# v of chunks 0 to 3 of batch 0 loaded through ScalarE's DMA queue instead of SyncE's

## The chip, the cores and the metric

The kernel runs on one NeuronCore of a Trainium2 chip. The core has TensorE (matrix products and transposes into PSUM), VectorE, ScalarE and GpSimd (elementwise work), and SyncE, which here only issues transfers. In the profile they are PE (PEld for its weight loads), DVE, ACT, POOL and SP. The metric is the device time of one execution in microseconds (us); lower is better.

## The reference

Four batches, eight heads, 768 tokens, head dimension 64; the heads side by side make rows of 512.

```python
gamma = 1.0 - 2.0 ** (-5.0 - np.arange(H))          # one decay per head
for t in range(S):
    state = gamma * state + einsum('bhd,bhe->bhde', k[:, :, t], v[:, :, t])
    y[:, :, t] = scale * einsum('bhd,bhde->bhe', q[:, :, t], state)
x = y.transpose(0, 2, 1, 3).reshape(B, S, H * D)
h = x.transpose(0, 2, 1) @ U @ V                    # rank 32, over tokens
u = x + h.transpose(0, 2, 1)
out = u + np.maximum(u @ w_ch1, 0.0) @ w_ch2        # 512 -> 2048 -> 512
```

A recurrent attention is followed by a low-rank mixing of tokens and a two-layer network on each token.

## The kernel before

The recurrence is computed in six chunks of 128 tokens (`NCK`). Within a chunk, q and k are scaled by powers of the decay (`ret_q0`, `ret_k`, giving `qd` and `kd` in bf16), transposed on TensorE (`ret_Tq0`, `ret_Tk0`), and multiplied to scores (`ret_S`), which VectorE masks (`ret_mask`). v is cast to bf16 by ScalarE (`ret_v`). `ret_sum` adds the chunk's k times v to the state in PSUM, `ret_state` takes a masked copy of it, and `ret_O` forms the chunk's output x from the masked scores with v and from the state with q. Then `mix_x`, `mix_P` and `mix_h` form u transposed, and `mlp1` and `mlp2` are the two layers.

For batches 1 to 3 the recurrence is woven into the two layers of the batch before. Batch 0 has nothing to be woven into: its recurrence stands in the open, in an order written out by hand in lines 574 to 649, with matmuls on zeros (`run_idle`) in places where TensorE would wait. `manual_schedule` keeps each engine's instructions in the order of the source. Each engine takes its own in order.

What the change and the prediction touch:

- Lines 178 to 188: SyncE issues batch 0's loads in the order k0, q0, k1, q1, k2, V, k3, v0, q2, k4, v1, k5, v2, v3, v4, v5, U. `k`c and `v`c are chunk c (256 KB each); `q`i is a pair of chunks (512 KB), so q0, q1, q2 of this list are chunks 0 and 1, 2 and 3, 4 and 5. V is moe_V and U moe_U, 96 KB each.
- `load_one` (line 136) makes the tile and issues the load. The pool `rin` has six buffers for each of k, q and v, so that batch 0's loads wait for no buffer.
- `ret_Tk0` (line 334) transposes the scaled k of a chunk; ScalarE copies the result out of PSUM as `kT` for chunks 0 to 3 and VectorE for 4 and 5. `ret_Tq0` (line 316) does so for a pair of q; of the first pair VectorE copies one half and ScalarE the other, of the later pairs ScalarE copies both in one instruction. Both copies by ScalarE have line 312.
- `ret_v` (line 274) casts v of a chunk on ScalarE; it waits for that v.
- Line 613: a small copy on GpSimd from v of chunk 4 stands ahead of the weight loads in GpSimd's own queue, so that these start when v4 has landed.

Of the kernel before, what the change touches and what calls it, by code (L numbers as in the profile page):

```python
# [47 lines left out]
def kernel(  # L48
# [11 lines left out]
    nc = tc.nc  # L60
    P = 128
# [28 lines left out]
    def bank(i, dtype=fp32, free=DM):  # L90
        n_bank[0] += 1
        return psum.tile([P, free], dtype, tag=f"bk{i}", name=f"bk{i}_{n_bank[0]}")
# [21 lines left out]
    def matmul(o, l, r, cols, **kw):  # L114
        nc.tensor.matmul(o, l, r, **kw)  # L115
        bal.mm(cols)
# [15 lines left out]
    staged = {}  # L132

    gate = (1, 0)

    def load_one(t, b, c, src, nm):
        n = rin.tile([P, H, D], fp32, tag=nm, name=f"{nm}_{b}_{c}")
        if (b, c) == gate:
            nc.scalar.activation(n[:, 0, :1], lsc, AF.Copy)
        nc.sync.dma_start(out=n, in_=src[b, :, ts(c, P), :].rearrange("h p d -> p h d"))  # L140
        t[nm, c] = n

    def load_chunk(b, c):
        t = {}
        for src, nm in ((k, "k_n"), (q, "q_n"), (v, "v_n")):
            load_one(t, b, c, src, nm)
        staged[b, c] = (t["q_n", c], t["k_n", c], t["v_n", c])
# [23 lines left out]
    t0 = {}  # L171

    def load_q0(i):
        t0["q", i] = q0f[:, i]
        nc.sync.dma_start(out=q0f[:, i].rearrange("p h e d -> p h (e d)"),
                          in_=q[0, :, ds(2 * P * i, 2 * P)].rearrange("h (p e) d -> p h (e d)", e=2))

    for what in ("k0", "q0", "k1", "q1", "k2", "V", "k3", "v0", "q2", "k4", "v1", "k5", "v2", "v3",
                 "v4", "v5"):
        if what == "V":  # L180
            nc.sync.dma_start(out=Vf, in_=moe_V)
        elif what[0] == "q":
            load_q0(int(what[1]))
        else:
            load_one(t0, 0, int(what[1]), k if what[0] == "k" else v, what[0] + "_n")
    for c in range(NCK):
        staged[0, c] = (None, t0["k_n", c], t0["v_n", c])
    nc.sync.dma_start(out=Uf, in_=moe_U.rearrange("(j p) r -> p j r", p=P))


# [3 lines left out]
    def run_idle(n):  # L194
        w = bank(0)
        for _ in range(n):
            matmul(w, idle[:, :P], idle, DM, start=True, stop=True)
# [50 lines left out]
    def cast_v():  # L248
        nc.vector.tensor_copy(out=Vs, in_=Vf)
# [8 lines left out]

    xs, rc = {}, {}
    st_p = {}  # L260

    def ret_k(b, c, eng):
        q_n, k_n, v_n = staged.pop((b, c))
        kd = rmid.tile([P, H, D], bf16, tag="kd", name=f"kd_{b}_{c}", bufs=6)
        eng.tensor_tensor(kd, k_n, Gk[:, c].unsqueeze(2).to_broadcast([P, H, D]), op=ALU.mult)  # L265
        rc[b, c] = dict(kd=kd, q_n=q_n, v_n=v_n)
# [22 lines left out]
    def by_dma(b):  # L289
        return b >= 2  # L290
# [11 lines left out]
    def ret_q0(i, eng):  # L302
        t0["qd", i] = []
        for e in (0, 1):
            d = rmid.tile([P, H, D], bf16, tag="qd", name=f"qd0_{i}_{e}", bufs=4)
            eng[e].tensor_tensor(d, t0["q", i][:, :, e],  # L306
                                 Gq0[:, 2 * i + e].unsqueeze(2).to_broadcast([P, H, D]), op=ALU.mult)
            t0["qd", i].append(d)

    def copy_by(eng, o, i):  # L310
        if eng == "A":
            nc.scalar.activation(o, i, AF.Copy)  # L312
        else:
            nc.vector.tensor_copy(out=o, in_=i)

    def ret_Tq0(i, bks, between=0):

        tp = [bank(bk, bf16, 2 * DM) for bk in bks]
        o = q0T[:, :, ds(2 * P * i, 2 * P)].rearrange("p n (t e) -> p e n t", e=2)
        for e, d in enumerate(t0["qd", i]):  # L320
            t = tp[e % len(tp)]
            if e and between:
                run_idle(between)
            for n in range(NP):
                nc.tensor.transpose(t[:, ds((e if len(tp) == 1 else 0) * DM + n * P, P)],
                                    d[:, ds(2 * n, 2)], ident)
                bal.mm(P)
        if len(tp) == 2:
            for e, eng in ((0, "V"), (1, "A")):
                copy_by(eng, o[:, e], tp[e][:, :DM].rearrange("p (n t) -> p n t", n=NP))  # L330
        else:
            copy_by("A", o, tp[0].rearrange("p (e n t) -> p e n t", e=2, n=NP))

    def ret_Tk0(c, eng="A"):
        r = rc[0, c]
        o = rmid.tile([P, NP, P], bf16, tag="qkT", name=f"kT_0_{c}", bufs=6)
        tp = bank((2, TP)[c % 2], bf16, 2 * DM)[:, :DM]
        for p in range(NP):
            nc.tensor.transpose(tp[:, ts(p, P)], r["kd"][:, ds(2 * p, 2)], ident)
            bal.mm(P)  # L340
        r["kT"], r["qT"] = o, q0T[:, :, ts(c, P)]
        copy_by(eng, o.rearrange("p n t -> p (n t)"), tp)
# [14 lines left out]
    def ret_S(b, cs, masks=True, bks=(SA, SB)):  # L357

        for c, bks in zip(cs, (bks, (OB, TP if by_dma(b) else 2))):
            r = rc[b, c]  # L360
            r["s"] = [bank(i) for i in bks]
            for p in range(NP):
                for e in (0, 1):
                    matmul(r["s"][e][:, ts(p, P)], r["kT"][ds(D * e, D), p],
                           r["qT"][ds(D * e, D), p], 80, start=True, stop=True)
        for c in cs:
            rc[b, c]["a"] = rmid.tile([P, 2, NP, P], bf16, tag="a", name=f"a_{b}_{c}", bufs=5)
            for e in (0, 1) if masks else ():
                ret_mask(b, c, e)

    def ret_mask(b, c, e):
        r = rc[b, c]
        nc.vector.tensor_tensor(r["a"][:, e], r["s"][e].rearrange("p (n t) -> p n t", n=NP), mask4,  # L373
                                op=ALU.mult)
        bal.book("V", 0.69)
# [196 lines left out]
    G, V = nc.gpsimd, nc.vector  # L572

    ret_k(0, 0, G)
    ret_Tk0(0)
    run_idle(6)
    ret_q0(0, (V, G))
    ret_Tq0(0, (1, OB), 3)
    run_idle(3)
    ret_k(0, 1, G)  # L580
    ret_q0(1, (G, V))
    ret_Tk0(1)
    ret_S(0, [0])
    run_idle(4)
    ret_Tq0(1, (1,))
    ret_k(0, 2, G)
    ret_Tk0(2)
    ret_S(0, [1], bks=(OB, ST))
    cast_v()
    run_idle(4)  # L590
# [128 lines left out]
```

## Time and profile before

| what | us |
|---|---|
| median of 3 runs | 229.44 |
| lowest, highest run | 229.36, 230.59 |
| span of the profiled execution | 227.7 |
| TensorE busy in the span | 220.0 |
| ScalarE busy | 114.0 |
| VectorE busy | 82.3 |
| GpSimd busy | 55.4 |

The span runs from the first to the last instruction in the trace; the profiled execution has no other time of its own, and the median of the runs lies 1.74 us above its span. SPq is SyncE's sequencer, which issues the loads: the length of an SPq row is the time that the issue held it, not the transfer. The time from the issue's start to the landing of the data stands in the view of transfers. A row of a timeline has start, length, engine, line, operation, output and inputs, count, and in brackets the idle time of the engine before it with what ended that.

### The profile page before, as it was taken

Reading aid. Unit: us, or ns where it says so; the run is one execution under the profiler, and the core shown is the slowest. Engines: PE = TensorE matmul, PEld = TensorE weight load, DVE = VectorE, ACT = ScalarE, POOL = GpSimd, SP = SyncE. Lnnn points to the kernel's source line nnn. Section 1 sums busy time; section 2 is a strip of 40 time slices with the busy share of each in tenths; the row PEclk is TensorE's granted clock in tenths of the full one; section 3 lists DMA queues with packets and bytes.
Section 4 is the critical chain, followed back from the end, with each engine's and each line's share of the span. In section 5 each row is a group of like instructions: output and inputs, shape, how many; then the busy total and the mean of one; then the engine's idle time right before and its main releaser. Section 6 shows DMA issues by size and latency. Waiting matters only on the chain.

```text
span 227.7 us, 4234 instructions
## 1 busy us (share of the span) xinstructions
PE 220.0 (97%) x1713; PEld 123.9 (54%) x1713; DVE 82.3 (36%) x155; ACT 114.0 (50%) x219; POOL 55.4 (24%) x63
## 2 busy tenths in 40 slices
PE   7898899999999999999999999999999999999995
PEld 2455666655566456656554445655554456654454
DVE  5587620003776440015673710035674510001221
ACT  4366777761336377767232627767134457770000
POOL 3852910026655330522035501050000000000000
DMA  7999899999999997987599959859311550001122
GB/s 177 241 242 202 112 193 206 201 208 228 219 210 270 211 243 188 196 168 100 105 236 236 250 132 217 202 101 94 94 49 46 135 146 0 0 0 49 61 79 92
DMA packets 102324, 34.95 MB, mean 154 GB/s; under 512 B 91264, under 2 KB 99328, under 8 KB 102304
## 3 DMA queue, kind: packets, MB, share of 16 engines
q1 hardware_dynamic: 97552, 30.49, 63.9%
q0 software_dynamic: 4752, 4.19, 11.7%
q8 instruction: 13, 0.21, 0.4%
q14 instruction: 7, 0.06, 0.1%
HBM read 27.46 MB, written 6.29 MB: 148 GB/s over the span
## 4 chain that ended last, share of the span: by engine, by line
PE 77%; SPq 7%; DMA 7%; DVE 3%; ACT 1%; issue 1%; POOL 1%; POOLq 0%
PE bk L115 75%; SPq L140 3%; DMA q0f<-in_q_dram 3%; SPq L296 2%; DMA qkT<-kd 2%; DVE a L373 1%; PE bk L351 1%; DMA qkT<-qd 1%; DMA uT<-x 1%; SPq L520 1%; DVE res L517 1%; DVE state L417 1%; POOL qd L306 1%; ACT q0T L312 1%; POOL kd L265 1%
## 5 line engine op out<-in xcount | busy, mean ns | idle before, releaser
L115 PE MATMUL bk<-w2b,gT 128*128 128x512 bf16 (+2 forms) x416 | 92.0, 363 | 0.0
L115 PE MATMUL bk<-uT,w1b 128*128 128x384 bf16 x512 | 84.5, 326 | 0.5 <-DMA uT<-x 0.5
L120 ACT ACTIVATE gT<-bk 128x384 bf16<-128x384 f32 x126 | 61.7, 490 | 31.8 <-PE bk L115 31.7
L115 PEld LDWEIGHTS <-w1b 128*128 128x128 bf16 x512 | 49.8, 98 | 34.3 <-issue 1.5
L115 PEld LDWEIGHTS <-gT 128*128 128x128 bf16 x416 | 37.9, 98 | 37.8 <-issue 0.8
L373 DVE TENSOR_TENSOR a<-bk,mask 128x512 bf16<-128x512 f32 x48 | 30.1, 683 | 40.4 <-PE bk L115 40.2
L265 POOL TENSOR_TENSOR kd<-k_n,Gk 128x512 bf16<-128x512 f32 x24 | 25.0, 1042 | 79.9 <-PE bk L115 47.2
L517 DVE TENSOR_TENSOR res<-bk,res 128x512 f32<-128x512 f32 (+2 forms) x17 | 10.7, 626 | 44.9 <-PE bk L115 44.9
L395 ACT ACTIVATE x<-bk 128x512 bf16<-128x512 f32 x23 | 13.7, 595 | 25.2 <-PE bk L115 25.2
L270 POOL TENSOR_TENSOR qd<-q_n,Gq 128x512 bf16<-128x512 f32 x18 | 18.7, 1042 | 10.5 <-DMA qkT<-qd 9.3
L417 DVE TENSOR_TENSOR state<-bk,bmask 128x512 bf16<-128x512 f32 x20 | 13.8, 691 | 12.5 <-PE bk L115 12.4
L276 ACT ACTIVATE vb<-v_n 128x512 bf16<-128x512 f32 x24 | 14.6, 623 | 2.2 <-DMA v_n<-in_v_dram 2.2
L115 PE MATMUL bk<-idle 128*128 128x512 bf16 x41 | 12.4, 430 | 1.2 <-DVE idle L192 1.2
L484 DVE TENSOR_TENSOR res<-bk,x 128x512 f32<-128x512 f32 x15 | 9.7, 686 | 8.0 <-PE bk L115 8.0
L486 ACT ACTIVATE x<-res 128x512 bf16<-128x512 f32 x15 | 9.3, 630 | 6.8 <-DVE res L484 6.5
L115 PEld LDWEIGHTS <-qkT 64*128 64x128 bf16 (+1 forms) x204 | 8.4, 95 | 7.4 <-issue 3.2
L124 DVE COPY qkT<-bk 128x1024 bf16<-128x1024 bf16 x3 | 2.1, 692 | 26.4 <-PE bk L351 26.4
L115 PE MATMUL bk<-vb,a 128*128 128x64 bf16 x192 | 9.5, 193 | 0.0
L115 PE MATMUL bk<-P_sb,Vb 128*128 128x512 bf16 x24 | 9.1, 380 | 0.0
L115 PE MATMUL bk<-vb,kd 128*128 128x128 bf16 x80 | 7.8, 219 | 1.2 <-DVE state L417 0.9
L120 ACT ACTIVATE qkT<-bk 128x1024 bf16<-128x1024 bf16 x3 | 3.1, 1023 | 11.3 <-PE bk L351 11.3
L115 PEld LDWEIGHTS <-a 128*128 128x128 bf16 x192 | 8.0, 98 | 0.6
(72 smaller groups left out, 104.9 us busy)
## 6 DMA issues: line engine op xcount, KB each, us to landing
k_n<-in_k_dram SPq DMA_DIRECT2D x24, 256.0 KB, 4.9
v_n<-in_v_dram SPq DMA_DIRECT2D x24, 256.0 KB, 5.1
out_dram<-res SPq DMA_DIRECT2D x23, 256.0 KB, 2.5
q_n<-in_q_dram SPq DMA_DIRECT2D x18, 256.0 KB, 5.0
w2b<-in_moe_w_ch_dram POOLq DMA_DIRECT2D x4, 512.0 KB, 17.3
q0f<-in_q_dram SPq DMA_DIRECT2D x3, 512.0 KB, 6.1
w1b<-in_moe_w_ch_dram POOLq DMA_DIRECT2D x3, 512.0 KB, 9.6
w1b<-in_moe_w_ch_dram POOLq DMA_DIRECT2D x2, 256.0 KB, 5.0
```

The source lines that it names most:

```text
L115: nc.tensor.matmul(o, l, r, **kw)
L120: nc.scalar.activation(o, i, AF.Relu if relu else AF.Copy)
L140: nc.sync.dma_start(out=n, in_=src[b, :, ts(c, P), :].rearrange("h p d -> p h d"))
L265: eng.tensor_tensor(kd, k_n, Gk[:, c].unsqueeze(2).to_broadcast([P, H, D]), op=ALU.mult)
L270: eng.tensor_tensor(qd, rc[b, c]["q_n"], Gq[:, c].unsqueeze(2).to_broadcast([P, H, D]), op=ALU.mult)
L276: nc.scalar.activation(vb, rc[b, c]["v_n"], AF.Copy)
L373: nc.vector.tensor_tensor(r["a"][:, e], r["s"][e].rearrange("p (n t) -> p n t", n=NP), mask4, op=ALU.mult)
L395: nc.scalar.activation(xs[b][:, c], o[0], AF.Copy)
L417: nc.vector.tensor_tensor(sb, ps.rearrange("p (n t) -> p n t", n=NP), bmask4, op=ALU.mult)
L484: nc.vector.tensor_tensor(u, h, xs[b][:, j], op=ALU.add)
L486: nc.scalar.activation(xs[b][:, j], u, AF.Copy)
L517: nc.vector.tensor_tensor(o, chp.pop((b, j)), o if by_token(b, j) else xs[b][:, j, ds(lo, w)], op=ALU.add)
```

## The change

`load_one` gets an argument for the engine that issues, SyncE if none is given. SyncE's list loses v0 to v3. A new function `load_v0(c)` issues v of chunk c on ScalarE and enters the tile where the later steps look for it. It is called at four places of the hand-written order. The bytes, the tiles and the arithmetic are the same.

```diff
-    def load_one(t, b, c, src, nm):
+    def load_one(t, b, c, src, nm, eng=nc.sync):
...
-        nc.sync.dma_start(out=n, in_=src[b, :, ts(c, P), :].rearrange("h p d -> p h d"))
+        eng.dma_start(out=n, in_=src[b, :, ts(c, P), :].rearrange("h p d -> p h d"))
...
-    for what in ("k0", "q0", "k1", "q1", "k2", "V", "k3", "v0", "q2", "k4", "v1", "k5", "v2", "v3",
-                 "v4", "v5"):
+    for what in ("k0", "q0", "k1", "q1", "k2", "V", "k3", "q2", "k4", "k5", "v4", "v5"):
...
-        staged[0, c] = (None, t0["k_n", c], t0["v_n", c])
+        staged[0, c] = (None, t0["k_n", c], t0.get(("v_n", c)))
...
+    def load_v0(c):
+        load_one(t0, 0, c, v, "v_n", nc.scalar)
+        if (0, c) in rc:
+            rc[0, c]["v_n"] = t0["v_n", c]
+        else:
+            staged[0, c] = (None, t0["k_n", c], t0["v_n", c])
...
     ret_k(0, 0, G)
     ret_Tk0(0)
+    load_v0(0)
     run_idle(6)
     ret_q0(0, (V, G))
     ret_Tq0(0, (1, OB), 3)
     run_idle(3)
+    load_v0(1)
     ret_k(0, 1, G)
     ret_q0(1, (G, V))
     ret_Tk0(1)
+    load_v0(2)
     ret_S(0, [0])
     run_idle(4)
     ret_Tq0(1, (1,))
     ret_k(0, 2, G)
     ret_Tk0(2)
+    load_v0(3)
     ret_S(0, [1], bks=(OB, ST))
```

The built program counts the landings of the hardware-issued loads with eight counters, given out in turn, and each load waits for the load before it on its counter. Of the built changed program, ScalarE's instructions from the first kT on, each with what it waits for (a DMAHW number is such a counter, PE is TensorE):

```
Activation kT chunk 0         waits PE
DMACopy v chunk 0             waits DMAHW4   (k of chunk 2)
Activation q0T, first pair    waits PE
DMACopy v chunk 1             waits DMAHW6   (k of chunk 3)
Activation kT chunk 1         waits PE
DMACopy v chunk 2             waits DMAHW7   (q2)
Activation q0T, second pair   waits PE
Activation kT chunk 2         waits PE
DMACopy v chunk 3             waits DMAHW0   (k of chunk 4)
Activation kT chunk 3         waits PE
Activation vb chunk 0         waits DMAHW4   (v of chunk 0)
```

What each number stands for at that point follows from the same program's other readers: GpSimd's scaling of k2 waits for DMAHW4, of k3 for DMAHW6, of q2 for DMAHW7, of k4 for DMAHW0. On SyncE k4, k5, v4, v5 and U wait for counters 0, 1, 2, 3 and 5, on which k0, q0, k1, q1 and V came before. In the program before, the first load that waits so is q2 (for k0), then k4 (q0), v1 (k1), k5 (q1), v2 (k2), v3 (V), v4 (k3), v5 (v0) and U (q2), all on SyncE.

## The prediction

> **What bounds the kernel now.** I read the page first, for how full TensorE is and where its gaps lie.
>
> ```profile
> span 227.7 us, 4234 instructions
> PE 220.0 (97%) x1713; PEld 123.9 (54%) x1713; DVE 82.3 (36%) x155; ACT 114.0 (50%) x219; POOL 55.4 (24%) x63
> PE   7898899999999999999999999999999999999995
> ```
>
> One slice is 5.7 us. TensorE is full from the sixth slice on, and the first five (28 us) hold the recurrence of batch 0 with nothing else to run: the only stage that the change touches. Next the chain of waits, over that stage (start us, us, what):
>
> ```profile
> 8.72 1.55 POOL qd L306
> 10.27 1.01 POOL kd L265
> ...
> 11.33 0.40 PE bk L339 x4
> 11.73 1.63 PE bk L115 x20
> 13.36 0.34 PE bk L339 x4
> 13.72 0.60 ACT kT L312
> 14.32 0.53 ACT vb L276
> ...
> 24.26 28.93 PE bk L115 x215
> ```
>
> So the stage is a chain of small steps across engines; from 24.26 us TensorE's own matmuls carry it. What delays the chain at 13.72 us and isn't caught up by 24.26 us lengthens the kernel by as much. Between the two the chain names engines only, no load: 24.26 - 13.72 = 10.5 us of compute in series. Now ScalarE's timeline, whose order the change edits:
>
> ```profile
> 5.46 0.60 ACT L312 ACTIVATE kT<-bk 128x512 bf16<-128x512 bf16 x1 [2.01 <-PE bk L339]
> 7.85 0.74 ACT L312 ACTIVATE q0T<-bk 128x512 bf16<-128x512 bf16 x1 [1.79 <-PE bk L325]
> 8.83 0.60 ACT L312 ACTIVATE kT<-bk 128x512 bf16<-128x512 bf16 x1 [0.24 <-PE bk L339]
> 10.99 1.31 ACT L312 ACTIVATE q0T<-bk 128x1024 bf16<-128x1024 bf16 x1 [1.56 <-PE bk L325]
> 12.16 0.58 ACT L312 ACTIVATE kT<-bk 128x512 bf16<-128x512 bf16 x1
> 13.72 0.60 ACT L312 ACTIVATE kT<-bk 128x512 bf16<-128x512 bf16 x1 [0.98 <-PE bk L339]
> 14.22 0.62 ACT L276 ACTIVATE vb<-v_n 128x512 bf16<-128x512 f32 x1
> ```
>
> These are, in order, kT of chunk 0, the second half of q0T's first pair (both above the chain's line but needed by it), kT1, q0T of the second pair, kT2, kT3, vb0. The issues of v0 to v3 come behind the first, second, third and fifth of them. TensorE's steps that hang on these evictions:
>
> ```profile
> 8.72 0.40 PE L115 MATMUL bk<-q0T,kT 64*128 64x128 bf16 x8
> 9.05 1.04 PE L115 MATMUL bk<-idle 128*128 128x512 bf16 x4
> 10.33 0.62 PE L325 MATMUL bk<-ident,qd 128*128 128x128 bf16 x8 [0.24 <-POOL qd L306]
> 12.96 0.40 PE L115 MATMUL bk<-q0T,kT 64*128 64x128 bf16 x8
> ```
>
> The scores of chunk 0 (8.72) start 0.13 us behind q0T's eviction (7.85 + 0.74). Those of chunk 2 (12.96) start 0.22 behind kT2's (12.16 + 0.58), and the transposes of chunk 3 and kT3 (13.72) follow.
>
> **The change, part by part.** The last views are SyncE's timeline, then the row of each issue (size, us from issue to landing) for k2, k3, v0, q2 and k4, in that order:
>
> ```profile
> 3.90 1.46 SPq L140 DMA_DIRECT2D k_n<-in_k_dram  x1
> 6.77 0.42 SPq L140 DMA_DIRECT2D k_n<-in_k_dram  x1
> 7.24 1.21 SPq L140 DMA_DIRECT2D v_n<-in_v_dram  x1
> 8.49 1.56 SPq L175 DMA_DIRECT2D q0f<-in_q_dram  x1
> 10.10 1.08 SPq L140 DMA_DIRECT2D k_n<-in_k_dram  x1
> ```
>
> ```profile
> k_n<-in_k_dram SPq DMA_DIRECT2D x1, 256.0 KB, 6.0
> k_n<-in_k_dram SPq DMA_DIRECT2D x1, 256.0 KB, 4.8
> v_n<-in_v_dram SPq DMA_DIRECT2D x1, 256.0 KB, 5.5
> q0f<-in_q_dram SPq DMA_DIRECT2D x1, 512.0 KB, 6.1
> k_n<-in_k_dram SPq DMA_DIRECT2D x1, 256.0 KB, 5.7
> ```
>
> Landings therefore: k2 at 3.90 + 6.0 = 9.9, k3 at 6.77 + 4.8 = 11.6, v0 12.7, q2 14.6, k4 15.8 us. 256 KB more in the queue is about 1.15 us (k3 to v0, k4 behind q2), 512 KB 1.85 (v0 to q2): the queue is full and lands at a steady rate.
>
> The added waits decide. In the built program (listed under the change) every load takes one of eight completion counters in turn and waits until that counter's earlier load has landed. On SyncE before, that wait had always been met. On ScalarE v0's issue waits for k2, v1's for k3, v2's for q2, v3's for k4, and behind the waiting issue stand evictions. That a ready instruction doesn't pass one that waits on ScalarE is in the rows above: v0 had landed at 12.7, ScalarE sat idle from 12.74 to 13.72 for TensorE, and vb0 still went after kT3.
>
> What an issue costs ScalarE no row shows, since only SyncE issues this way. Bounds:
>
> ```profile
> 0.74 0.45 SPq L140 DMA_DIRECT2D k_n<-in_k_dram  x1
> L140 SPq DMA_DIRECT2D v_n<-in_v_dram x6: 1071/1198/2404, 7.2 to 19.1; - x6
> ```
>
> 0.45 us is the first issue, into an empty queue; 2.40 the longest v load (third figure, in ns). I take their median, 1.2: ScalarE's queue holds little, but the transfer engines are as full as for those rows.
>
> - v0: waits to 9.9, ends 11.1. The q0T eviction, ready at 7.85, goes at 11.1: 3.25 us late. Chunk 0's scores go to 11.97, the idle matmuls behind them end 1.37 later, and the second pair's transposes at about 14.0. The next wait covers all of it.
> - v1: k3 lands at 11.6, issue to 12.8, kT1 to 13.4. Chunk 1's scores stand behind the 14.0 of TensorE: hidden.
> - v2: q2's landing ends the wait. SyncE now issues q2 at 7.24 in v0's place. With all of v0 behind q2 it lands at 14.6 - 1.15 = 13.45; with v0 and v1 both ahead, at 14.6 + 1.15 = 15.75. I take 14.6, as before: v0's bytes move in that time either way. The issue ends at 15.8, and q0T's second pair, 10.99 before, is 4.8 us late. TensorE's 14.0 is the cover of v0's stall: from an end of v2 before 14.0, v0's stall would set the delay.
> - v3: k4 landed at 15.8; with v1's 256 KB ahead 17.0; issue to 18.2. kT3 can't go before 13.72 + 4.8 = 18.5, so this wait has cover of 0.3 us; past that it adds directly.
> - Removed: SyncE's four v issues, so k4, k5, v4, v5 and U go out earlier. What that could give back is below, as a rival; vb1's wait for v1 isn't in the chain. w1, gated by v4's landing, starts no later. No arithmetic is added; what follows 24.26 us is shifted whole.
>
> On who gets the engines when two queues hold work, one stretch of the trace has two, 39 to 49 us (packets, MB, share):
>
> ```profile
> q0 software_dynamic: 1527, 1.51, 90.1%
> q1 hardware_dynamic: 2241, 0.57, 31.5%
> ```
>
> GpSimd's weights and SyncE's loads divide one capacity, unequally. So a second queue is not a second set of engines, and v0 does take from q2; how much is the 13.45 to 15.75.
>
> A rule that speaks against the change: the Trainium skill, "DMA: Bandwidth & Descriptors", section "Issuing engines are not separate DMA queues", says that loads issued from several engines share the same 16 and that only issue time is saved. The stretch agrees in that both queues slow each other; by the rule q2 and v0 together end no sooner than 14.6, by the rows one may end at 13.45.
>
> Sum: 14.6 + 1.2 - 10.99 = 4.8 us. The span of 227.7 becomes 232.5; the median run, 229.44, lies 1.74 above the span, so **234.2 us**. Ends: 13.45 + 0.45 - 10.99 = 2.9, giving 232.4; 15.75 + 2.40 - 10.99 = 7.2, giving 236.6.
>
> **Rivals.**
>
> A, not slower: the waiting issue doesn't hold the evictions behind it (or the waits are met by the time ScalarE comes to them). Then only SyncE's earlier loads count. Past 13.72 us TensorE's idle time on a load is the wait for kd5, that is k5:
>
> ```profile
> 20.63 0.40 PE L339 MATMUL bk<-ident,kd 128*128 128x128 bf16 x4 [0.57 <-POOL kd L265]
> ```
>
> At most 0.57 us is won: 228.9 to 229.4 us. It decides if ScalarE runs q0T near 7.85 and 10.99 us. Against it: vb0's order, and 9.9 and 14.6 lying 2 and 3.6 us past those evictions' times.
>
> B, the issue is cheap and q2 lands early: the forecast's low end, 232.4. For it: ScalarE's queue is empty. Against it: the full transfer engines.
>
> C, ScalarE's issue also waits out one that SyncE has in hand: 1.2 + 1.2 = 2.4 us instead of 1.2, the second pair at 14.6 + 2.4 = 17.0, 6.0 late: 235.4 us. For it: from 6.77 us on SyncE's rows follow one another without a pause, and they would still at 14.6, since the full queue sets their rate. Against it: no row shows the two engines holding each other up. The Trainium skill, "Perfetto Trace Analysis", the part on hardware-generated DMA instructions, states such a lock (the generator is held for exclusive use); no run here shows it yet.
>
> D, the stall lets TensorE's clock fall. The first matmuls ran at 3.84 / 9 = 0.43 us each and the later at 1.46 / 6 = 0.24:
>
> ```profile
> 1.19 3.84 PE L115 MATMUL bk<-idle 128*128 128x512 bf16 x9 [1.19 <-DVE idle L192]
> 5.26 1.46 PE L115 MATMUL bk<-idle 128*128 128x512 bf16 x6
> ```
>
> TensorE would sit idle from 8.8 to 12.0 us and again before chunk 2's scores. Were it slow for another 3.84 us at half speed behind the second gap, that loses up to 1.9: 236.1 us. Against it: idle matmuls stand between the gaps. The Trainium skill, "TensorE: Matmul & The Clock Gate", Part 1, sets a full idle window of about 3.4 us as the condition; no gap of that length stands in the rows above.
>
> **How the numbers follow.** The forecast with q2 near 14.6 and an issue near 1.2 has 0.52, B 0.14, C 0.15, D 0.10, A 0.09. The range, 231.4 to 237.2, holds all but A and a tail on top; the likeliest case alone is 233 to 236. A measurement of this kernel tells 0.5% (1.15 us) from no change, and A's 0.09 divides into 0.03 faster and 0.06 same; all the rest is slower, 0.91.
>
> **What would show it.** ScalarE's timeline after: q0T's first eviction near 11.1 us instead of 7.85, its second near 15.8 instead of 10.99, kT3 near 18.5, with ScalarE idle until loads land or issuing. v2's issue should stand at q2's landing, and the chain's long TensorE piece should start near 29.1 instead of 24.26. Wrong if these evictions keep their times; wrong in size if an issue takes far from 1.2 us, if q2 lands outside 13.45 to 15.75, or if v3's wait outlasts 18.5.

## The result and the profile after

| | median us | lowest to highest | runs |
|---|---|---|---|
| before | 229.7 | 229.36 to 230.59 | 4 |
| after | 232.32 | 231.91 to 233.12 | 4 |

The ratio is 1.0121, with a 95% interval of 1.0089 to 1.0152: the change makes the kernel 1.2% slower, some 2.6 us. The profiled execution of after has a span of 230.1 us, 2.4 more than before's. Of its page, TensorE's row and the granted clock, in tenths of each of 40 slices:

```profile
PE   7598799999999999999999999999999999999995
PEclk9979999999999999999999999999999999999999
```

The loss is where the prediction looked: slice 2 (6 to 11.5 us) is busy to 5 tenths where before had 8, and in slice 3 (to 17 us) TensorE's clock is down (before had it at 1.00 in all windows of the stage). ScalarE's timeline, ACTq being its own issues:

```profile
10.28 0.50 ACTq L140 DMA_DIRECT2D v_n<-in_v_dram  x1
10.82 0.74 ACT L318 ACTIVATE q0T<-bk 128x512 bf16<-128x512 bf16 x1 [4.56 <-DMA k_n<-in_k_dram]
11.80 0.39 ACTq L140 DMA_DIRECT2D v_n<-in_v_dram  x1
12.23 0.60 ACT L318 ACTIVATE kT<-bk 128x512 bf16<-128x512 bf16 x1 [0.67 <-PE bk L115]
13.66 0.83 ACTq L140 DMA_DIRECT2D v_n<-in_v_dram  x1
14.73 1.32 ACT L318 ACTIVATE q0T<-bk 128x1024 bf16<-128x1024 bf16 x1 [1.90 <-PE bk L331]
15.16 1.74 ACTq L140 DMA_DIRECT2D v_n<-in_v_dram  x1
15.90 0.59 ACT L318 ACTIVATE kT<-bk 128x512 bf16<-128x512 bf16 x1
17.31 0.60 ACT L318 ACTIVATE kT<-bk 128x512 bf16<-128x512 bf16 x1 [0.82 <-PE bk L345]
```

The first eviction of q0T goes at 10.82 instead of 7.85, and the bracket names what ended ScalarE's 4.56 us of idling: the landing of a k. It needs no k; v0's issue ahead of it does, by its counter. The second eviction goes at 14.73 instead of 10.99, kT3 at 17.31 instead of 13.72. TensorE around the two evictions, and the windows (stretch, its length, busy us and count of PE, PEld, DVE, ACT and POOL, then clock, DMA share and GB/s):

```profile
11.61 0.40 PE L115 MATMUL bk<-q0T,kT 64*128 64x128 bf16 x8 [2.64 <-ACT q0T L318]
11.95 1.89 PE L115 MATMUL bk<-idle 128*128 128x512 bf16 x4
13.63 1.06 PE L331 MATMUL bk<-ident,qd 128*128 128x128 bf16 x8
```

```profile
10.00:12.00 2.00, 0.39 (x9) 0.28 (x9) 0.00 (x0) 0.74 (x1) 1.60 (x3) 0.99 1.26 236
12.00:14.00 2.00, 2.00 (x9) 0.90 (x9) 1.29 (x2) 0.60 (x1) 1.09 (x2) 0.50 1.28 256
14.00:16.00 2.00, 2.00 (x22) 1.45 (x20) 0.39 (x1) 1.27 (x2) 1.89 (x2) 0.66 1.38 218
```

Behind 2.64 us of idling TensorE runs at half clock: the transposes of the second pair take 1.06 us where before they took 0.62. v2's issue ended at 13.66 + 0.83 = 14.49; the eviction behind it still waited to 14.73 for these slow transposes. The chain of waits, cut:

```profile
3.93 6.33 DMA k_n<-in_k_dram
10.28 0.50 ACTq L140
10.82 0.75 ACT q0T L318
...
17.31 0.60 ACT kT L318
...
27.72 28.93 PE bk L115 x215
```

k2's load, v0's issue on ScalarE and the eviction behind it now stand in the chain, where before had steps of GpSimd and TensorE. q2's load and v2's issue are not in it. From kT3 to the long piece it takes 10.4 us, as before (10.5). The long piece starts 3.46 us late, of which the span shows 2.4. Where the rest went is seen at two steps of TensorE past 130 us, of before and then of after:

```profile
133.65 17.75 PE L115 MATMUL bk<-uT,w1b 128*128 128x384 bf16 x108 [0.46 <-DMA uT<-x]
158.54 0.93 PE L115 MATMUL bk<-qkT 64*128 64x128 bf16 x16
```

```profile
136.49 17.71 PE L115 MATMUL bk<-uT,w1b 128*128 128x384 bf16 x108
161.34 0.62 PE L115 MATMUL bk<-qkT 64*128 64x128 bf16 x16
```

Before waited 0.46 us for a transposed u, and its scores at 158.54 took 0.31 longer; after does neither. The two kernels stand 3.46 us apart at the long piece, 2.84 at the first of these rows and 2.80 at the second, whose longer run takes it to 2.49, and so to the end.

### The profile page after: what moved, and what is told of

Its sections match the earlier page's. It is cut to its first block, busy times and chain, and to the rows that moved or that the text cites. A ratio compares the mean times of both kernels' runs of the same rounds, so it can differ in the third digit from the quotient of the medians.

```text
span 230.1 us, 4232 instructions
## 1 busy us (share of the span) xinstructions
PE 221.3 (96%) x1713; PEld 125.2 (54%) x1713; DVE 82.3 (36%) x155; ACT 113.8 (49%) x219; POOL 55.7 (24%) x63
## 3 DMA queue, kind: packets, MB, share of 16 engines
q0 software_dynamic: 4752, 4.19, 11.6%
## 4 chain that ended last, share of the span: by engine, by line
PE 90%; DMA 3%; DVE 3%; ACT 1%; SPq 1%; issue 1%; ACTq 0%
PE bk L115 88%; DMA k_n<-in_k_dram 3%; PE bk L357 1%; DVE a L379 1%; ACT q0T L318 1%; SPq L175 1%; SPq L140 1%; PE bk L331 1%; DVE state L423 0%; DVE res L523 0%; PE bk L345 0%; DVE qd L312 0%; ACT kT L318 0%; DVE uT L124 0%; ACT vb L282 0%
## 5 line engine op out<-in xcount | busy, mean ns | idle before, releaser
L115 PE MATMUL bk<-idle 128*128 128x512 bf16 x41 | 13.4, 459 | 1.2 <-DVE idle L191 1.2
L120 ACT ACTIVATE qkT<-bk 128x1024 bf16<-128x1024 bf16 x3 | 3.1, 1025 | 12.7 <-PE bk L357 12.7
```

The costliest lines, as they stand in the source:

```text
L120: nc.scalar.activation(o, i, AF.Relu if relu else AF.Copy)
```

## The experiments

Times are compared with runs of before on the same chip, whose medians were 229.09 (the first four kernels below), 229.11 (the next four), 229.02 (the three after) and 229.34 us (the last). "Long piece" is the start of TensorE's long piece in the one profiled execution.

| kernel | median us | ratio, 95% interval | long piece | span |
|---|---|---|---|---|
| waits_only | 233.15 | 1.0174 (1.0134 to 1.0214) | 29.28 | 231.7 |
| waits_met | 230.99 | 1.0085 (1.0060 to 1.0109) | 26.81 | 229.7 |
| gaps | 230.87 | 1.0073 (1.0047 to 1.0098) | 26.68 | 229.1 |
| warm | 233.14 | 1.0163 (1.0136 to 1.0190) | 27.22 | 230.9 |
| after_again | 232.05 | 1.0119 (1.0078 to 1.0161) | 28.28 | 230.7 |
| wait_k2 | 231.89 | 1.0102 (1.0050 to 1.0153) | 27.34 | 229.7 |
| wait_q2 | 234.45 | 1.0210 (1.0138 to 1.0282) | 30.13 | 232.6 |
| delay | 233.06 | 1.0174 (1.0123 to 1.0226) | – | 231.0 |
| gaps01 | 230.08 | 1.0045 (1.0021 to 1.0069) | 25.29 | 227.7 |
| wait_k2_warm | 232.04 | 1.0130 (1.0112 to 1.0147) | 26.91 | 230.3 |
| before_again | 229.22 | 1.0011 (0.9995 to 1.0027) | 24.35 | 227.4 |
| late12 | 230.41 | 1.0049 (1.0033 to 1.0064) | 25.44 | 228.6 |

A caution on single profiles: q0T's first eviction, where nothing stands in its way, went between 7.85 us (before) and 8.78 (wait_q2) although the programs are the same up to there. Differences of starts below about 0.9 us are not read here as effects.

**Waits without the second queue (waits_only).** Before, with all loads on SyncE, and at the four places of the change a copy of one column from the tile whose landing the issue waits for:

```diff
+    def wait_for(i, t):
+        nc.scalar.activation(hold[:, i : i + 1], t, AF.Copy)
...
+    wait_for(0, t0["k_n", 2][:, 0, :1])
...
+    wait_for(1, t0["k_n", 3][:, 0, :1])
...
+    wait_for(2, t0["q", 2][:, 0, 0, :1])
...
+    wait_for(3, t0["k_n", 4][:, 0, :1])
```

> The kernel before, with all loads on SyncE, and four tiny copies on ScalarE (128x1) at the places of the four issues, each of which reads the load that the counter of that issue would wait for: k2, k3, q2, k4. Nothing is issued by ScalarE. Theory (the waits hold the evictions): q0T's first eviction at about 10.2 us (k2 lands at 9.9, a copy is 0.2), its second at about 14.8 (q2 lands at 14.6), TensorE's long piece from about 28.1 instead of 24.26; about 1 us of that comes back later, so that the span is near 230.5 and the ratio to before near 1.012. Rival (the second queue or the time of the issues costs it): q0T's evictions near 7.9 and 11.0 and a ratio within 0.3% of 1.

ScalarE's timeline of waits_only:

```profile
10.30 0.20 ACT L577 ACTIVATE hold<-k_n 128x1 f32<-128x1 f32 x1 [3.94 <-DMA k_n<-in_k_dram]
15.22 0.20 ACT L577 ACTIVATE hold<-q0f 128x1 f32<-128x1 f32 x1 [2.77 <-DMA q0f<-in_q_dram]
15.32 1.29 ACT L312 ACTIVATE q0T<-bk 128x1024 bf16<-128x1024 bf16 x1
```

The waits alone, with no issue and no second queue, cost 4.1 us, more than the change itself and more than the theory's 1.012. So they are enough for the loss. Here q2 stands behind v0 in SyncE's queue and lands at 15.2 instead of after's 13.6, and the second eviction follows it, 0.6 us later than after's. Another 1.0 us came behind kT3: from there to the long piece it takes 11.4 us, against 10.4 in after, and TensorE's clock, 1.00 in 16 to 18 us, is down again in 18 to 20, at 0.81. That the change gains by having q2 ahead of v0 fits the 0.6 us and was not tried by itself.

**One wait at a time (wait_k2, wait_q2).** The first of the four copies alone, and the third alone.

> The kernel before with one tiny copy on ScalarE, behind kT0, that reads k2: v0's wait alone, nothing else moved. Theory (v0's wait alone costs most of it, because TensorE's clock falls behind it): q0T's first eviction at 10.2 to 10.5, granted clock near 0.5 in 12 to 14 us, second eviction at 14.0 to 14.4, TensorE's long piece at 27.0 to 27.5, ratio 1.010 to 1.014. Rival (only v2's wait counts): second eviction at 13.2 or before, long piece at 26.5 or before, ratio under 1.009.

> The kernel before with one tiny copy on ScalarE, behind kT1, that reads q2: v2's wait alone. q2 lands at 14.6 to 15.2 here, since SyncE issues v0 ahead of it. Theory: q0T's first eviction on time (7.9), its second at 14.8 to 15.4, TensorE's long piece at 28.1 to 28.7 (or more by what the clock loses while TensorE waits from about 12 to 16), ratio 1.012 to 1.018. So either wait alone costs what both together cost. Rival (the waits add up): long piece at about 26, half of the whole.

ScalarE of wait_k2 (q0T's two evictions), then of wait_q2 (the copy, with the second eviction right behind it at 15.02):

```profile
10.55 0.72 ACT L312 ACTIVATE q0T<-bk 128x512 bf16<-128x512 bf16 x1
13.77 1.31 ACT L312 ACTIVATE q0T<-bk 128x1024 bf16<-128x1024 bf16 x1 [2.05 <-PE bk L325]
```

```profile
14.91 0.20 ACT L577 ACTIVATE hold<-q0f 128x1 f32<-128x1 f32 x1 [4.66 <-DMA q0f<-in_q_dram]
```

Either wait alone is all of the change's loss of 2.6 us or more, in the medians: 2.8 us for k2's, 5.3 for q2's, the second past its theory. In wait_q2 some 1.8 us of that came behind kT3 (12.35 us from there to the long piece, 10.5 in before), with the clock at 0.50 from 18 to 22 us, behind 2.99 us of idling. The waits don't add, since the stall of the first passes while the second's load is still under way. In after q2 lands early, and the two waits are nearly worth the same: v2's issue ends 0.2 us before TensorE is ready from the first stall.

**The same queues, with loads that have landed (waits_met).** After, with SyncE's later loads placed further down in the source, so that the counters fall otherwise: v0's issue now waits for k0, v1's for q1, v2's for k2 and v3's for q2.

```diff
-    for what in ("k0", "q0", "k1", "q1", "k2", "V", "k3", "q2", "k4", "k5", "v4", "v5"):
+    def load_sync(*whats):
...
+    load_sync("k0", "q0", "k1", "q1", "k2", "V", "k3")
...
     load_v0(0)
+    load_sync("q2")
...
     load_v0(1)
+    load_sync("k4", "k5")
...
     load_v0(2)
+    load_sync("v4", "v5")
...
     load_v0(3)
+    load_u()
```

> The changed kernel, the four issues at the same places of ScalarE's order, but q2, k4, k5, v4, v5 and U stand later in the source, so that the counters are dealt out otherwise: v0 waits for k0 (landed near 4 us), v1 for q1 (8.7), v2 for k2 (9.9), v3 for q2 (13.6). Theory: q0T's evictions at 7.9 to 8.6 and 11.0 to 11.6 us, only v3's wait can hold kT3, by about 0.5; TensorE's long piece from 24.3 to 25.3, ratio 1.000 to 1.004. Rival (second queue or issue time): q0T's second eviction still past 13 and a ratio above 1.008. A third possibility: v0, now issued near 4 us, takes the engines from q1, which then lands up to 1.2 us past 8.7 and delays everything by that, ratio near 1.004.

ScalarE of waits_met, and GpSimd's scaling of k3:

```profile
5.68 0.43 ACTq L140 DMA_DIRECT2D v_n<-in_v_dram  x1
8.40 0.75 ACT L322 ACTIVATE q0T<-bk 128x512 bf16<-128x512 bf16 x1 [2.13 <-PE bk L335]
11.40 1.31 ACT L322 ACTIVATE q0T<-bk 128x1024 bf16<-128x1024 bf16 x1 [1.29 <-PE bk L335]
15.13 0.37 ACTq L140 DMA_DIRECT2D v_n<-in_v_dram  x1
15.55 0.60 ACT L322 ACTIVATE kT<-bk 128x512 bf16<-128x512 bf16 x1 [2.39 <-PE bk L115]
```

```profile
13.33 1.04 POOL L275 TENSOR_TENSOR kd<-k_n,Gk 128x512 bf16<-128x512 f32 x1 [1.65 <-DMA k_n<-in_k_dram]
```

Both evictions of q0T are back within 0.6 us of before's: with their waits met, the issues of v0 to v2 hold nothing. A loss of 1.9 us stays, more than the theory allowed. v0, issued at 5.68, shares the transfer engines with k3, which lands at 13.3 instead of 11.6; and v3's issue, which waits for q2, holds kT3 to 15.55. Behind kT3 the clock is down in this profile:

```profile
16.00:18.00 2.00, 1.29 (x17) 0.61 1.37 218
18.00:20.00 2.00, 2.00 (x15) 0.54 1.34 222
```

But seven of the ten runs kept a clock of 1.00, and their median, 230.80, is still 1.7 us above before. So the second queue seems to have a price of its own; this run does not part it from v3's wait.

**Other places, with issues one eviction later (gaps).** After, v0 to v2 each one eviction further down, the counters so that v0 waits for q1, v1 for k2, v2 for V and v3 for k3. v3's place behind kT2 is the same as in after, not one later as the expectation has it.

```diff
+    load_sync("k0", "q0", "k1", "q1", "k2", "V", "k3", "q2")
...
     ret_Tk0(0)
-    load_v0(0)
...
     ret_Tq0(0, (1, OB), 3)
     run_idle(3)
-    load_v0(1)
+    load_sync("k4", "k5", "v4")
+    load_v0(0)
...
     ret_Tk0(1)
-    load_v0(2)
+    load_v0(1)
...
     ret_Tq0(1, (1,))
+    load_v0(2)
     ret_k(0, 2, G)
     ret_Tk0(2)
     load_v0(3)
+    load_sync("v5")
...
+    load_u()
```

> ScalarE still issues v0 to v3, but each one eviction later, and the loads stand in the source so that v0 waits for q1 (8.7 us), v1 for k2 (9.9), v2 for V (10.4), v3 for k3 (11.6): each wait ends before the next eviction is ready. Theory: q0T's evictions keep 7.9 and 11.0, ratio 0.998 to 1.002, since the chain of the first stage is compute; v0 lands near 14.5 and may hold vb0 by 0.3. Rival (second queue): k3, q2 or k5 land later and the ratio is above 1.004.

ScalarE of gaps:

```profile
10.50 0.44 ACTq L140 DMA_DIRECT2D v_n<-in_v_dram  x1
11.41 1.32 ACT L322 ACTIVATE q0T<-bk 128x1024 bf16<-128x1024 bf16 x1 [1.24 <-PE bk L335]
11.41 2.14 ACTq L140 DMA_DIRECT2D v_n<-in_v_dram  x1
13.62 2.27 ACTq L140 DMA_DIRECT2D v_n<-in_v_dram  x1
15.94 0.60 ACT L322 ACTIVATE kT<-bk 128x512 bf16<-128x512 bf16 x1 [1.74 <-PE bk L115]
```

No wait holds q0T now. What holds kT2 (to 13.60) and kT3 (to 15.94) is the issue itself: v2's takes 2.14 us and v3's 2.27, where v1's took 0.44. The ratio is the rival's, but its cause isn't: behind 11.41 us the chain holds 0.83 and 1.70 us of these two issues and no load.

**The slow clock (warm, wait_k2_warm).** After, and wait_k2, each with twelve idle matmuls in the gap ahead of chunk 0's scores:

```diff
+    run_idle(12)
     ret_S(0, [0])
```

> The changed kernel with 12 more matmuls on zeros between the transposes of k1 and chunk 0's scores, where TensorE stood idle from 8.9 to 11.6 us and its granted clock then fell to 0.50. Theory (v2's wait for q2 is as long as v0's stall with the slow clock): the clock stays 1.00, the transposes of q's second pair end near 13.7 instead of 14.69, but q0T's second eviction goes at the end of v2's issue, 14.5 instead of 14.73; gain at most 0.2 us, ratio to before still 1.011 to 1.012. Rival (the slow clock carries the loss): that eviction at 13.7, gain 1.0 us, ratio near 1.008.

> The wait for k2 alone, with 12 more idle matmuls that keep TensorE's clock up through the gap. Theory (of the 3.1 us that this wait cost, some 0.4 to 0.6 was TensorE at half clock behind the gap): clock 1.00 in every stretch, q0T's second eviction 13.2 to 13.5 instead of 13.77, kT3 16.4 to 16.6 instead of 16.92, long piece 26.7 to 26.9 instead of 27.34, ratio near 1.008. Rival (the stall is passed on whole and the clock costs nothing): 27.3 and 1.010, or more where the idle matmuls delay chunk 0's scores.

ScalarE of warm, then of wait_k2_warm:

```profile
14.22 1.32 ACT L318 ACTIVATE q0T<-bk 128x1024 bf16<-128x1024 bf16 x1 [1.66 <-PE bk L345]
```

```profile
13.91 1.32 ACT L312 ACTIVATE q0T<-bk 128x1024 bf16<-128x1024 bf16 x1 [2.05 <-PE bk L325]
```

The clock stays at 1.00 in both. In warm v2's issue, which ends at 14.18, decides the second eviction, 0.5 us earlier than in after, and the long piece starts 0.5 earlier; in wait_k2_warm it starts 0.43 earlier than in wait_k2, though the second eviction, expected at 13.2 to 13.5, came at 13.91 behind the added matmuls. Both gains lie below the 0.9 us of the caution, and after_again's long piece starts 0.56 later than after's, so what the slow clock costs the change is not shown. The time gained nothing (1.0163 and 1.0130, no lower than the kernels without the idle matmuls): the profiles waited 0.9 and 0.6 us for a transposed u, near 90 and 141 us, where after and wait_k2 waited for none. The runs of the change, after and after_again, don't show it either: two of eight kept a clock of 1.00 and took 232.06 and 232.09 us, the others (0.991 to 0.993) 231.78 to 233.12. It is clearer where the clock stayed down longer: of wait_q2's four runs the one at 0.993 took 232.65 us, those at 0.984 and 0.985 took 234.44 to 235.35.

**Is a delay given back later? (delay, after_again, before_again).** Before with sixteen idle matmuls, 3.45 us of them, ahead of the two layers; and both kernels once more, unchanged.

```diff
+    run_idle(16)
+
     for b in range(B):
```

> The kernel before with 16 more matmuls on zeros (0.216 us each, 3.45 in all) between batch 0's recurrence and the first layer: a delay of TensorE and of nothing else. If the later stages give back part of any delay, because SyncE's transposes of u and of q, k are paced by transfers and not by TensorE, the time grows by 2.4 to 2.8 us (ratio 1.0105 to 1.012) and TensorE waits nowhere behind 32 us; if what came back was chance, by 3.2 to 3.7 (1.014 to 1.016).

> The changed kernel once more, beside the runs below. Expected as its first profile: q0T's evictions near 10.8 and 14.7 us, TensorE's long piece from 27.2 to 27.8, ratio to before 1.010 to 1.017. Open is what the later stages do: in the first profile TensorE waited nowhere behind 28 us, in that of before 0.46 us for a transposed u at 133 us. If the change itself removes that wait, it is absent again and the span is 202.4 us longer than the long piece's start; if it varies by itself, it may be there.

> The kernel before, unchanged, for a second profile of its tail. Theory (that a delay seemed to come back behind 130 us is chance of the one profile of before, which waited 0.5 us for a transposed u and lost 0.5 at other places): long piece again near 24.3 us, and from it to the end about 202.4 us and not 203.4; ratio 1.000. Rival (a late start of the long piece is given back by a wait that it covers): 203.0 to 203.4 us from the long piece to the end again.

The delay of 3.45 us costs 3.95 in the medians, 2.8 to 5.2 by the interval: nothing comes back. After_again repeats the ratio; its evictions of q0T (11.47 and 15.02) and its long piece came 0.3 to 0.7 us later than after's. Before_again, TensorE past 130 us:

```profile
133.47 17.74 PE L115 MATMUL bk<-uT,w1b 128*128 128x384 bf16 x108 [0.19 <-DMA uT<-x]
158.36 0.87 PE L115 MATMUL bk<-qkT 64*128 64x128 bf16 x16
```

From the long piece to the end it takes 227.4 - 24.35 = 203.05 us, between the theory's 202.4 and first profile's 203.4. Both profiles of before lose something there, and both of after, at 202.4, nothing. But warm and wait_k2_warm, later than before by 3.0 and 2.7 us, lose more (203.7 and 203.4). That stretch takes 202.4 to 203.7 us over all profiles, and what decides is left open; it is not simply given back to whoever comes late.

**ScalarE issuing without its waits or a full queue (gaps01, late12).** Gaps with only v0 and v1 on ScalarE; then v1 and v2 alone, behind q0T's second eviction and kT2, with v0, q2, k4 and k5 ahead on SyncE. The second edit, of late12:

```diff
+    load_sync("k0", "q0", "k1", "q1", "k2", "V", "k3", "v0", "q2", "k4", "k5")
...
     ret_Tq0(1, (1,))
+    load_v0(1)
     ret_k(0, 2, G)
     ret_Tk0(2)
-    load_v0(3)
+    load_v0(2)
+    load_sync("v3", "v4", "v5")
```

> Only v0 and v1 are issued by ScalarE, v0 behind q0T's first eviction and v1 behind kT1, with waits for loads that have landed by then (k1 and q1); v2 to v5 and U are SyncE's again, behind k5. Theory (waits cost, and issues with several transfers of ScalarE's queue in flight cost; an issue into a nearly empty queue costs 0.4 us and is hidden): q0T's evictions near 7.85 and 11.2 us, kT3 13.7 to 14.2, the long TensorE piece near 24.3 to 24.8, ratio 0.998 to 1.003. Rival (the second queue itself costs, by pushing back k3, q2 and k4): kT3 past 14.7 us because the loads of chunk 3 or of the second pair are late, ratio 1.005 and over.

> Only v1 and v2 are issued by ScalarE, behind q0T's second eviction and behind kT2; v0, q2, k4 and k5 stand on SyncE as before and ahead of them, and both waits (for q1 and k2) have been met by then. Theory (what costs is a wait that holds evictions, an issue into a queue that still holds two transfers, and a load that is pushed back, not ScalarE as issuer): both issues near 0.4 us, q0T's evictions and kT3 within 0.2 us of before's two profiles (7.85 to 8.02, 10.99 to 11.12, 13.72 to 13.87), long TensorE piece 24.2 to 24.6, ratio 0.998 to 1.002. Rival (an issue on ScalarE, or its queue beside SyncE's, costs in itself): long piece at 24.8 us or later, ratio 1.003 and over, the loss found where a load of chunks 3 to 5 lands late.

Of gaps01 ScalarE's cast of v0, and VectorE's qd with GpSimd's kd of chunks 4 and 5:

```profile
14.88 0.63 ACT L286 ACTIVATE vb<-v_n 128x512 bf16<-128x512 f32 x1 [0.28 <-DMA v_n<-in_v_dram]
```

```profile
17.79 1.15 DVE L316 TENSOR_TENSOR qd<-q0f,Gq 128x512 bf16<-128x512 f32 x1
```

```profile
17.34 2.49 POOL L275 TENSOR_TENSOR kd<-k_n,Gk 128x512 bf16<-128x512 f32 x2 [2.32 <-DMA k_n<-in_k_dram]
```

The issues are short (v0's 0.49, v1's 0.37) and kT3 is in place at 14.01, as the theory had it; but v0 lands at 14.9 instead of 12.7 and vb0 waits for it, and k4 at 17.3 instead of 15.8, so that kd4 falls beside VectorE's qd and qd takes 1.15 us, against 0.68 in before_again. The ratio, 1.0045, lies between theory and rival. Late12 then tells them apart. Its chain:

```profile
11.97 8.66 DMA k_n<-in_k_dram
...
25.44 28.93 PE bk L115 x215
```

k5, issued at 11.97 between v1 and v2 on the other queue, lands at 20.6 and stands in the chain, and its scaling ends at 21.76. In the kernel before, where SyncE issued it at 12.55, k5's scaling was done by 20.63, where the transposes behind it started. kT3 at 14.38 was late too, but so was q0T's first eviction (8.72), ahead of any edit. With nothing held on ScalarE (both issues took about 0.4 us, at 11.64 and 12.42) the ratio is 1.0049: the theory falls, the rival holds. No kernel tried here beats before.

## Why the prediction was right, and where its sizes were off

The forecast was 234.2 us in 231.4 to 237.2; the runs gave 232.32, inside the range but below the 233 to 236 of its likeliest case. The mechanism is shown by two edits from opposite sides: the waits alone bring the loss (waits_only), and waits for landed loads put q0T's evictions back (waits_met). The forecast had v2's wait end 1.8 us behind v0's stall (15.8 against TensorE's 14.0); the two came out within 0.2 us of each other. Rival A, that the waiting issue holds nothing, falls with the same rows.

The sum was 14.6 + 1.2 - 10.99 = 4.8. By its terms, in the profile of after:

- "I take 14.6, as before": this step failed most. v2's issue starts at 13.66, close to the bound of 13.45 that stood for all of v0 behind q2. "v0's bytes move in that time either way" was wrong: by v0's issue at 10.28 q2 had been under way for 3 us (SyncE issued it at 7.31), and v0's landing moved to 16.1 instead. -0.9 us.
- The price of an issue, "their median, 1.2", measured 0.50, 0.39, 0.83 and 1.74; the one in the sum 0.83. -0.4.
- "TensorE's 14.0 is the cover of v0's stall": TensorE was ready at 14.69, not 14.0, through the slow clock, and decided over v2's issue. So in after v0's wait for k2 set the delay, where the prediction had v2's for q2. In after_again v2's issue ended last, 0.2 us behind TensorE, and yet its chain, too, goes by k2's load, v0's issue and TensorE's slow matmuls. With the clock at 1.00, in warm, v2's issue decided. +0.2.
- v3 has "cover of 0.3 us": its issue ran 15.16 to 16.90, and kT3 waited for TensorE to 17.31. It cost nothing, as forecast.
- From the second eviction to the long piece, 0.3 was absorbed, 3.74 becoming 3.46.
- "What follows 24.26 us is shifted whole" failed in these profiles by 1.0 us, past 130 us. Delay shows that it holds for a delay as such; the stretch varies by 1.3 us between profiles for a reason left open.

4.8 - 0.9 - 0.4 + 0.2 - 0.3 - 1.0 = 2.4, the difference of the spans.

Rival B's number, 232.4, was met, but not by its conditions alone: q2 did land near its low end, while v2's issue was not at 0.45 and the second eviction came 3.74 us late, not 2.9; the rest of the way to B's time is the stretch past 130 us. Rival C falls: v1's issue took 0.39 us while SyncE was issuing without a pause:

```profile
11.68 3.97 SPq L140 DMA_DIRECT2D v_n<-in_v_dram  x2
```

The lock that the Trainium skill states in "Perfetto Trace Analysis", in the part on hardware-generated DMA instructions, is not contradicted, since it can be held for less than a row's length, but no row shows ScalarE waiting out an issue of SyncE's. Rival D came true in kind, behind the first gap, not behind the second, and what it cost the change is not shown: up to 0.5 us in two pairs of profiles, less than single profiles differ by. In wait_q2, with the clock at 0.50 from 18 to 22 us, some 1.8 us came behind kT3. The Trainium skill, "TensorE: Matmul & The Clock Gate", Part 1, asks for an idle window of about 3.4 us; here the clock was at 0.50 behind a row's 2.64 us of idling in after, and at 0.59 behind 2.14 in wait_k2:

```profile
11.32 0.40 PE L115 MATMUL bk<-q0T,kT 64*128 64x128 bf16 x8 [2.14 <-ACT q0T L312]
```

```profile
12.00:14.00 2.00, 2.00 (x16) 0.59 1.16 276
```

The trace does not agree that only a gap as long as the window slows the clock, and the measurement decides. No safe length comes out of it: in waits_met the clock fell with no gap above 1.03 us in the 8 us before it, and in gaps one of 1.27 left it at 1.00. The Trainium skill, "DMA: Bandwidth & Descriptors", section "Issuing engines are not separate DMA queues", has the loads of all issuing engines run on the same 16 engines. The traces of waits_met, gaps01 and late12 agree: what moves to the second queue takes from k3 (13.3 instead of 11.6), k4 (17.3 instead of 15.8) and k5 (20.6 instead of 19.5).

## What to carry to other kernels

A load issued by an engine that also computes is an instruction of that engine: read in the built program what its issue waits for, by name and landing time, and what stands behind it, before asking what the issue itself costs. Where the transfer engines are full, the order of one queue is the order of need; a second queue lets a load that is wanted later take capacity from one that is wanted sooner, and that cost 0.5% here even with no wait left. A start that moves by less than a microsecond in one profile is no effect until a second profile of the unchanged program has shown how far that start moves by itself.

## What was not expected of the hardware

- ScalarE's queue behaves as if it held two such loads. Rows of v0 and v1 in after, us from issue (10.28 and 11.80) to landing last; in gaps these are 6.0 and 7.0 (issued at 9.10 and 10.50):

```profile
v_n<-in_v_dram ACTq DMA_DIRECT2D x1, 256.0 KB, 5.8
v_n<-in_v_dram ACTq DMA_DIRECT2D x1, 256.0 KB, 6.7
```

  In after v0 lands at 16.1 and v2's issue ends at 14.49, 1.6 us ahead; v1 lands at 18.5 and v3's issue ends at 16.90, 1.6 ahead. In gaps v0 lands at 15.1 and v2's ends at 13.55; v1 at 17.5 and v3's at 15.89: 1.6 again, both times. Where that moment is past (waits_met), or fewer than two of ScalarE's loads are under way, an issue takes 0.37 to 0.50. Of eight such rows in four profiles (after, after_again, warm, gaps) seven lie between 1.55 and 1.66 us and one at 1.97; it was not tried by itself.
- An issue goes when the instructions ahead of it have had their waits met, not when they are done: in gaps q0T's second eviction and v2's issue both start at 11.41; in after v3's issue starts at 15.16, ahead of kT2 at 15.90, which stands before it in the program.
- VectorE's qd of 128x512 took 0.68 us alone (before_again) and 1.15 beside GpSimd's kd, whose two took 2.49 where one alone takes 1.04.
